# Threshold attention and an FNet mix on one core: the last 64 queries' scores in four 64x64 tiles, and the sequence transform's sine and cosine rest as two row tiles

## The chip, the cores and the metric

The kernel runs on one core of one Trainium2 chip, as one launch. The metric is the device time of that core in microseconds (us); lower is better. TensorE is called PE, VectorE DVE, ScalarE ACT, GpSimd POOL and SyncE SP, as the profile does. PE loads of stationary operands are listed apart, as PEld.

## The reference, cut to what matters

All tensors are fp32. `q`, `k` and `v` are (8 batches, 8 heads, 576 positions, 64); `tau` is 0.02.

```python
scores = (1 / sqrt(64)) * q @ k.T
scores = where(scores >= max(scores) - tau, scores, -1e9)
attn = exp(scores - max(scores));  attn = attn / (sum(attn) + 1e-9)
x = (attn @ v), heads side by side            # (8, 576, 512)
u = x + real(fft(fft(x, axis=1), axis=2))      # over the sequence, then over the features
ch = relu(layernorm(u) @ w_ch1) @ w_ch2        # 512 -> 2048 -> 512
return u + ch
```

## The kernel before, in words

There is no scheduler: every instruction stands in its engine's queue in the order in which the Python code issues it, and the code interleaves three streams by hand.

**Attention.** Two heads form a pair, 4 pairs to a batch, 32 in all. A pair's queries are taken in five steps `t` of a global index `i = 5 n + t`: four steps of 128 queries for each head, and a fifth (`t == 4`) with the last 64 queries of both heads. A step runs `scores` (PE), a softmax (DVE maximum `neg`, ACT exponential and threshold `thr`, DVE mask-and-sum, DVE `inverse`, and scaling by `den`), and one step later `weights_in_parts`, which transposes the weights `e` on PE into `pe` and `pw` and copies them by ACT into `ends` and `e_t`. At the steps 3 and 1 (of the next pair) `values_in_parts` multiplies by `v`. The first batch uses `step`, the second `second_batch`, and the other six a loop at the end with `softmax_first`, `softmax_second` and `softmax_third`. `prep_pair` transposes a pair's keys and queries on DVE at `t == 3` of the pair before; `prep_ends` fills `q_ends` on POOL; `load_v` loads the values by SP.

In the steps 0 to 3 the two heads lie on partitions 0 to 63 and 64 to 127 of `kT` and `qT`. A head's product contracts over 64 rows, so that it is a row tile, written 64*128 in the profile. In the first batch the four products of a step are issued head by head, later head 0 and head 1 in turns. In the fifth step `q_ends` is a 128x128 block diagonal of both heads' 64 queries, and its two products (one for each half of the keys) use the whole array (128*128).

Scores lie in PSUM in tiles `sc` of two banks, from a ring of two such tiles; all other PE results take one bank each from a ring of four, `mm`.

**Mixing.** `fold_rows` and `partial_sums` prepare the Fourier transform. `mixing(b)` then makes, for `u` in 0, 1, 2 (128, 48 and 128 sequence rows), the feature transforms `py`, evicted by ACT into `y_e` (cosine) and `y_o` (sine). `over_seq` then transforms over the sequence, in four products each: two with 128 rows of `y[:, 0]` and `y[:, 2]`, and two with the rest `y[:, 1]`, of which only 33 rows are not zero. For each of two column blocks `t`, ACT copies the sine side to `tmp`, and DVE makes the sum and the difference with the cosine side. `mixing` is a generator: each `yield` ends a piece.

**Channel product.** `channels` (the first group of 512 rows) and `two_level` (Strassen-like, the other eight) are generators too. `fill` takes pieces of them by a budget, and one piece of `mixing` by `mix(1)`, between the parts of an attention step. The last batch's mixing and the last two groups run after all attention has ended.

Each program matmul in fp32 that is no transpose leaves two MATMUL records and two LDWEIGHTS records in the trace.

Of the kernel before, what the change touches and what calls it, by code (L numbers as in the profile page):

```python
# [47 lines left out]
def kernel(  # L48
# [18 lines left out]
    NT = 5  # L67
# [75 lines left out]
    def load_v(n):  # L143

        b, p = n // NPAIR, PAIRS[n % NPAIR]
        vt = v_in[n % 2]
        for j in range(2):
            h = 2 * p + (j + p) % 2
            nc.sync.dma_start(
                out=vt[:, j:8:2, :], in_=v[b, h, 0:512, :].rearrange("(t p) d -> p t d", p=128)  # L150
            )
            nc.sync.dma_start(out=vt[64 * j : 64 * j + 64, 8 + j, :], in_=v[b, h, 512:576, :])
# [12 lines left out]
    for u in range(2):  # L165
        for j in range(2):
            nc.gpsimd.memset(v_in[u][64 - 64 * j : 128 - 64 * j, 8 + j, :], 0.0)


    q_ends = const.tile([128, 128], FP32, name="q_ends")  # L170
    nc.gpsimd.memset(q_ends[:, :], 0.0)
# [29 lines left out]
    seq_xe = const.tile([128, 2, NE], FP32, name="seq_xe")  # L201
    seq_xo = const.tile([128, 2, NO], FP32, name="seq_xo")


    SEQ = (
        (((0, 1, 128),), seq_even, 0, ((0, 128),)),
        (((0, 16, 128),), seq_odd, 1, ((0, 128),)),
        (((0, 129, 16), (16, 0, 1)), seq_xe, 0, ((0, 17),)),
        (((32, 0, 16),), seq_xo, 1, ((32, 16),)),
    )  # L210

    def load_seq():
        for u, (pieces, dst, parity, parts) in enumerate(SEQ):
            for p, r, n in pieces:
                nc.sync.dma_start(out=f[p : p + n, u, 0 : 2 * KH], in_=dft_seq[r : r + n, :])
            if dst is seq_xo:
                nc.sync.dma_start(out=f[32:33, u, KH : 2 * KH], in_=dft_seq[144:145, KH : 2 * KH])

    def copy_seq():
        nc.gpsimd.memset(seq_xe[:, :, :], 0.0)  # L220
        nc.gpsimd.memset(seq_xo[:, :, :], 0.0)
        for u, (pieces, dst, parity, parts) in enumerate(SEQ):
            for p, n in parts:
                for c in range(2):
                    nc.gpsimd.tensor_copy(
                        dst[p : p + n, c, :], f[p : p + n, u, KH * c + parity : KH * (c + 1) : 2]
                    )
        nc.gpsimd.memset(f[:, :, 145:160], 0.0)
        nc.gpsimd.memset(f[:, :, FW + 143 : FW + 160], 0.0)
# [153 lines left out]
    def inverse(i, nh):  # L383
        den = sb.tile([128, 2], FP32, tag="den", bufs=3, name="den")
        nc.vector.tensor_reduce(
            out=den[:, 0:nh], in_=den_eps[i % 3][:, 0:nh, :], axis=AXIS_X, op=ALU.add
        )
        nc.vector.reciprocal(den[:, 0:nh], den[:, 0:nh])  # L388
        return den

    heads = {}
    steps = {}
    xs = {}
# [7 lines left out]
    def prep_pair(n):  # L401

        q_raw, k_raw = loaded.pop(n)
        kT = sb.tile([128, D + S], FP32, tag="kT", name="kT")
        nc.vector.transpose(kT[:, D : D + S], k_raw[:, :])
        nc.vector.transpose(kT[64:128, 0:D], k_raw[64:128, 512:S])
        qT = sb.tile([128, S], FP32, tag="qT", bufs=1, name="qT")  # L410
        nc.vector.transpose(qT[:, :], q_raw[:, :])
        heads[n] = (qT, kT, v_in[n % 2])
        if n + 1 < B * NPAIR and not late:
            load_pair(n + 1)

    def prep_ends(n):

        for j in range(2):
            hp = slice(64 * j, 64 * j + 64)
            nc.gpsimd.tensor_copy(q_ends[hp, hp], heads[n][0][hp, 512:S])  # L420
# [6 lines left out]
    def scores(i):  # L427
# [3 lines left out]
        nh = 2 if t < 4 else 1  # L431
        sc = [ps.tile([128, 2, 512], FP32, tag="sc", name=f"sc{j}") for j in range(nh)]
        if t < 4:
            order = [(c, j) for c in range(2) for j in range(2)]
            if i < per_batch:
                order.sort(key=lambda cj: cj[1])
            for c, j in order:
                if True:
                    hp, k0 = slice(64 * j, 64 * j + 64), D * (1 - j)
                    nc.tensor.matmul(  # L440
                        sc[j][:, c, 0:HALF], qT[hp, 128 * t : 128 * t + 128],
                        kT[hp, k0 + HALF * c : k0 + HALF * (c + 1)], start=True, stop=True,
                    )
        else:
            for c in range(2):
                nc.tensor.matmul(  # L446
                    sc[0][:, c, 0:HALF], q_ends[:, :], kT[:, D + HALF * c : D + HALF * (c + 1)],
                    start=True, stop=True,
                )
        steps[i] = (sc, nh)  # L450

    def softmax(i, between=None, meanwhile=None, behind=None):


        t = i % NT
        sc, nh = steps[i]
        neg = sb.tile([128, 2], FP32, tag="neg", bufs=3, name="neg")
        thr = sb.tile([128, 2], FP32, tag="thr", bufs=3, name="thr")
        e = sb.tile([128, 2 * S], FP32, tag="e", name="e")
        for j in range(nh):  # L460
            nc.vector.tensor_reduce(  # L461
                out=neg[:, j : j + 1], in_=sc[j][:, :, 0:HALF], axis=AXIS_XY, op=ALU.max,
                negate=True,
            )
        if meanwhile is not None:
            meanwhile()
        for j in range(nh):
            ej = e[:, S * j : S * (j + 1)].rearrange("p (c n) -> p c n", c=2)
            nc.scalar.activation(
                out=ej, in_=sc[j][:, :, 0:HALF], func=ACT.Exp, bias=neg[:, j : j + 1], scale=1.0  # L470
            )
            if j == 0:
                nc.scalar.activation(
                    out=thr[:, 0:nh], in_=neg[:, 0:nh], func=ACT.Identity,
                    bias=thr_off[:, :], scale=-1.0,
                )
            nc.vector.scalar_tensor_tensor(  # L477
                out=ej, in0=sc[j][:, :, 0:HALF], scalar=thr[:, j : j + 1], in1=ej,
                op0=ALU.is_ge, op1=ALU.mult, accum_out=den_eps[i % 3][:, j, 0:1],
            )  # L480
# [4 lines left out]
        den = inverse(i, nh)  # L485
# [3 lines left out]
        if normalized(i // NT):  # L489
            nc.vector.tensor_scalar(  # L490
                out=e[:, 0:S], in0=e[:, 0:S], scalar1=den[:, 0:1], scalar2=None, op0=ALU.mult
            )
            if nh == 2:
                nc.scalar.activation(
                    out=e[:, S : 2 * S], in_=e[:, S : 2 * S], func=ACT.Copy, scale=den[:, 1:2]
                )
            steps[i] = (e, None)
        else:
            steps[i] = (e, den[:, 0:nh])

    def spread_inverse(i):
        e, den = steps[i]
        if i % NT == 4:
            nc.scalar.copy(e[:, S : S + 64], e[:, 512:S])
        if den is None:
            return
        nh = den.shape[1]
        rec = sb.tile([128, 2 * D], FP32, tag="rec", name="rec")
        nc.scalar.copy(
            rec[:, :].rearrange("p (j d) -> p j d", j=nh), _repeated(den, 2 * D // nh)  # L510
        )
        steps[i] = (e, rec)

    def softmax_first(i):
        sc, nh = steps[i]
        neg = sb.tile([128, 2], FP32, tag="neg", bufs=3, name="neg")
        thr = sb.tile([128, 2], FP32, tag="thr", bufs=3, name="thr")
        e = sb.tile([128, 2 * S], FP32, tag="e", name="e")
        for j in range(nh):
            nc.vector.tensor_reduce(  # L520
                out=neg[:, j : j + 1], in_=sc[j][:, :, 0:HALF], axis=AXIS_XY, op=ALU.max,
                negate=True,
            )
        for j in range(nh):
            ej = e[:, S * j : S * (j + 1)].rearrange("p (c n) -> p c n", c=2)
            nc.scalar.activation(  # L526
                out=ej, in_=sc[j][:, :, 0:HALF], func=ACT.Exp, bias=neg[:, j : j + 1], scale=1.0
            )
            if j == 0:
                nc.scalar.activation(  # L530
                    out=thr[:, 0:nh], in_=neg[:, 0:nh], func=ACT.Identity,
                    bias=thr_off[:, :], scale=-1.0,
                )
        steps[i] = (sc, nh, e, thr)

    def softmax_second(i):
        sc, nh, e, thr = steps[i]
        for j in range(nh):
            ej = e[:, S * j : S * (j + 1)].rearrange("p (c n) -> p c n", c=2)
            nc.vector.scalar_tensor_tensor(  # L540
                out=ej, in0=sc[j][:, :, 0:HALF], scalar=thr[:, j : j + 1], in1=ej,
                op0=ALU.is_ge, op1=ALU.mult, accum_out=den_eps[i % 3][:, j, 0:1],
            )
        steps[i] = (nh, e, inverse(i, nh))

    def softmax_third(i):
        nh, e, den = steps[i]
        for j in range(nh):
            nc.scalar.activation(  # L549
                out=e[:, S * j : S * (j + 1)], in_=e[:, S * j : S * (j + 1)], func=ACT.Copy,  # L550
                scale=den[:, j : j + 1],
            )
        if nh == 1:
            nc.scalar.copy(e[:, S : S + 64], e[:, 512:S])
# [6 lines left out]
    def weights_in_parts(i):  # L561
# [25 lines left out]
        nc.tensor.transpose(pe[:, 0, :], e[:, 512:640], ident[:, :])  # L587
# [6 lines left out]
        else:  # L594
            for j in range(2):
                hp = slice(64 * j, 64 * j + 64)
                nc.scalar.copy(ends[hp, 0:kept, q0 : q0 + 64], pe[hp, 0:kept, hp])
        qs = slice(q0, q0 + (128 if t < 4 else 64))
        for j in range(2 if t < 4 else 1):
# [3 lines left out]
            for c in range(4):  # L603
                c0 = (S + D) * j + 128 * c
# [3 lines left out]
            else:  # L608
                nc.scalar.copy(  # L609
                    e_t[:, :, qs].rearrange("p (j c) q -> p j c q", j=2),  # L610
                    pw[:, :, :].rearrange("p c (j q) -> p j c q", j=2),
# [1298 lines left out]
```

## Time and profile before

| | |
|---|---|
| time, three runs | 1544.44, 1545.87, 1548.71 us; median 1545.87 |
| the profiled execution: its own time | 1547.94 us |
| its span, first to last instruction | 1546.2 us |
| granted TensorE clock | 0.997 |
| busy: PE, PEld, DVE, ACT, POOL | 1524.0, 1186.0, 1063.2, 916.4, 779.4 us |
| PE groups the change touches: L440, L446 | 168.4 us in 1024 records, 36.3 us in 128 |
| L766 (`py`), L783 and L787 (`over_seq`) | 34.6 us in 240, 66.4 us in 320 |

"Busy" is the union of the records' durations. A matmul's record lasts longer than the time until the next can start, so that records overlap and a busy PE can still be slowed; what a piece of work costs PE is read from the start of its first record to the start of the next piece. "x8" in a line of the timeline merges eight records in a row; the time in brackets is idle time before the line and what ended it. The first batch of attention takes about 0 to 125 us, the second 125 to 320 us, and the others some 168 us each until 1313 us.

### The profile page before, as it was taken

To read this page: it belongs to the slowest core of one execution; us is meant where nothing else is said; L and a number is where in the kernel's file an instruction comes from. 1 tells how busy PE (TensorE), PEld (TensorE's weight loads), DVE (VectorE), ACT (ScalarE), POOL (GpSimd) and SP (SyncE) were. 2 spreads that over 40 slices of the span, in tenths; PEclk is the share of its full clock that TensorE was granted. 3 is DMA by queue.
4 is the path that set the end of the run, shared out by engine and by line. 5 is a ranking of instruction groups with operands and counts; after the bars stand their busy time and mean duration, and the time that the engine had idled before them with its cause. 6 is when DMAs were issued, how large, how long until landed. Compare 5 with 4: busy or idle time off the path is not lost.

```text
span 1546.2 us, 27021 instructions
## 1 busy us (share of the span) xinstructions
PE 1524.0 (99%) x9786; PEld 1186.0 (77%) x9786; DVE 1063.2 (69%) x2141; ACT 916.4 (59%) x1921; POOL 779.4 (50%) x964
## 2 busy tenths in 40 slices
PE   9999999999999999999999999999999999999999
PEld 5556555556788778887788878887788778989999
DVE  7977676846779466866578566956687657746546
ACT  6875676655666576656775666666665676133131
POOL 3775563034365642546255724554264625647635
PEclk9999999999999999999999999999999999999999
DMA  7423233465956354644455354635464534646655
GB/s 171 130 59 119 78 92 105 139 183 165 280 187 206 92 173 125 186 113 146 146 167 160 120 159 133 199 92 172 120 195 132 160 117 142 220 163 231 234 196 184
DMA packets 248907, 239.31 MB, mean 155 GB/s; under 512 B 197027, under 2 KB 218533, under 8 KB 228678
## 3 DMA queue, kind: packets, MB, share of 16 engines
q1 hardware_dynamic: 246262, 237.28, 50.1%
q8 instruction: 78, 1.28, 0.3%
q10 hardware_dynamic: 2512, 0.30, 0.1%
q14 instruction: 55, 0.45, 0.1%
HBM read 205.93 MB, written 31.46 MB: 154 GB/s over the span
## 4 chain that ended last, share of the span: by engine, by line
PE 91%; DVE 4%; ACT 2%; POOL 1%; DMA 1%; issue 0%; ACTq 0%; DVEq 0%; POOLq 0%
PE ph L1210 25%; PE po L1400 21%; PE pv L636 10%; PE sc L440 10%; PE pw L605 7%; PE po L933 4%; PE ph L909 3%; PE sc L446 2%; PE py L766 2%; PE pe L587 1%; PE pa L783 1%; PE pn L858 1%; PE pa L787 1%; PE pm L360 1%; PE po L1379 1%; DVE neg L461 1%
## 5 line engine op out<-in xcount | busy, mean ns | idle before, releaser
L520 DVE TENSOR_REDUCE neg<-sc 128x1 f32<-128x576 f32 x216 | 154.3, 751 | 117.1 <-PE sc L440 105.5
L526 ACT ACTIVATE e<-sc,neg 128x576 f32<-128x576 f32 x216 | 158.6, 734 | 114.3 <-DVE neg L520 114.3
L1147 DVE TENSOR_TENSOR hs<-ph,hs 128x512 f32<-128x512 f32 (+1 forms) x128 | 105.3, 823 | 167.1 <-PE ph L1210 97.3
L1400 PE MATMUL po<-w,w_all 128*128 128x128 f32 x1728 | 219.4, 276 | 0.0
L1400 PEld LDWEIGHTS po<-w,w_all 128*128 128x128 f32 x1728 | 205.4, 192 | 7.4 <-issue 4.0
L1156 POOL TENSOR_TENSOR w<-hs 128x512 f32<-128x512 f32 x32 | 42.1, 1317 | 312.3 <-ACT hs L1152 249.3
L540 DVE SCALAR_TENSOR_TENSOR e<-sc,thr,e 128x576 f32<-128x576 f32 x216 | 168.4, 812 | 27.2 <-ACT thr L530 27.1
L1210 PE MATMUL ph<-u_t,w 128*128 128x256 f32 x768 | 180.9, 382 | 0.6 <-DMA w<-f 0.6
L607 ACT COPY e_t<-pw 128x512 f32<-128x512 f32 x256 | 148.4, 594 | 44.2 <-PE pw L605 42.7
L440 PE MATMUL sc<-kT,qT 64*128 64x288 f32 x1024 | 168.4, 430 | 5.9 <-DVE e L477 5.5
L605 PE MATMUL pw<-ident,e 128*128 128x128 f32 x1152 | 169.3, 274 | 3.7 <-ACT ends L593 1.9
L549 ACT ACTIVATE e<-e,den 128x576 f32<-128x576 f32 x216 | 157.4, 774 | 2.9 <-DVE den L388 2.2
L1210 PEld LDWEIGHTS ph<-u_t,w 128*128 128x128 f32 x768 | 140.9, 190 | 23.6 <-issue 5.3
L1210 PE MATMUL ph<-w_all,w 128*128 128x256 f32 x672 | 157.1, 382 | 1.1 <-DVE w_all L1132 1.0
L605 PEld LDWEIGHTS pw<-ident,e 128*128 128x128 f32 x1152 | 135.8, 141 | 19.3 <-issue 5.6
L1263 POOL TENSOR_TENSOR w_all<-w_all 128x128 f32<-128x128 f32 (+2 forms) x160 | 121.7, 777 | 44.5 <-DVE w_all L1420 23.4
L1210 PEld LDWEIGHTS ph<-w_all,w 128*128 128x128 f32 x672 | 123.5, 190 | 23.9 <-issue 4.9
L1152 ACT ACTIVATE hs<-hs 128x512 f32<-128x512 f32 (+1 forms) x96 | 74.1, 772 | 113.8 <-DVE hs L1147 113.0
L440 PEld LDWEIGHTS sc<-kT,qT 64*128 64x128 f32 x1024 | 95.1, 186 | 55.4 <-issue 22.9
L1400 PE MATMUL po<-w,hs 128*128 128x128 f32 x912 | 119.8, 278 | 0.0
L1400 PEld LDWEIGHTS po<-w,hs 128*128 128x128 f32 x912 | 109.8, 192 | 9.5 <-issue 8.0
L636 PE MATMUL pv<-e_t,v_in 128*64 128x320 f32 (+1 forms) x512 | 72.1, 423 | 1.5 <-ACT e_t L609 0.8
(227 smaller groups left out, 2910.6 us busy)
## 6 DMA issues: line engine op xcount, KB each, us to landing
w<-f SPq DMA_DIRECT2D x150, 1024.0 KB, 4.9
hs<-in_moe_w_ch_dram SPq DMA_DIRECT2D x23, 512.0 KB, 4.7
q_in<-in_q_dram SPq DMA_DIRECT2D x128, 72.0 KB, 4.1
out_dram<-u SPq DMA_DIRECT2D x36, 256.0 KB, 2.5
k_in<-in_k_dram SPq DMA_DIRECT2D x124, 72.0 KB, 2.4
v_in<-in_v_dram SPq DMA_DIRECT2D x64, 128.0 KB, 5.1
f<-w SPq DMA_DIRECT2D x14, 512.0 KB, 3.3
f<-w SPq DMA_DIRECT2D x7, 1024.0 KB, 4.8
```

Source lines behind the costliest of these rows:

```text
L440: nc.tensor.matmul(sc[j][:, c, 0:HALF], qT[hp, 128 * t : 128 * t + 128], kT[hp, k0 + HALF * c : k0 + HALF * (c + 1)], start=True, stop=True,)
L520: nc.vector.tensor_reduce(out=neg[:, j : j + 1], in_=sc[j][:, :, 0:HALF], axis=AXIS_XY, op=ALU.max, negate=True,)
L526: nc.scalar.activation(out=ej, in_=sc[j][:, :, 0:HALF], func=ACT.Exp, bias=neg[:, j : j + 1], scale=1.0)
L540: nc.vector.scalar_tensor_tensor(out=ej, in0=sc[j][:, :, 0:HALF], scalar=thr[:, j : j + 1], in1=ej, op0=ALU.is_ge, op1=ALU.mult, accum_out ...
L549: nc.scalar.activation(out=e[:, S * j : S * (j + 1)], in_=e[:, S * j : S * (j + 1)], func=ACT.Copy, scale=den[:, j : j + 1],)
L605: nc.tensor.transpose(pw[:, c, :], e[:, c0 : c0 + 128], ident[:, :])
L607: nc.scalar.copy(e_t[:, 4 * j : 4 * j + 4, qs], pw[:, :, :])
L636: nc.tensor.matmul(pv[64 * j : 64 * j + 64, 0:m], vt[:, 2 * c + j, :], e_t[:, 4 * j + c, 0:m] if c < 4 else ends[:, 0, 0:m], start=(c == 0 ...
L1147: nc.vector.tensor_tensor(out=to, in0=bank, in1=to if other is None else other, op=ALU.add)
L1210: nc.tensor.matmul(bank[:, 256 * q : 256 * q + 256].rearrange("p (two n) -> p two n", two=2), left[:, 256 * c + 128 * q : 256 * c + 128 * ...
L1263: return lambda: eng.tensor_tensor(out=to, in0=to, in1=other, op=ALU.add)
L1400: nc.tensor.matmul(to, lefts[m][j][:, s], right_[:, 128 * s : 128 * (s + 1)], start=jn in (0, 4) and s == 0, stop=s == 3, skip_group_check ...
```

## The change

**The last 64 queries.** `q_ends` holds both heads' 64 queries one above the other, without the diagonal. Its four products, head `j` by key half `c`, each use 64 rows and 64 columns of the array and write partitions 64c to 64c + 63 of bank `j`. A query's scores are then in two halves on two partitions, so that maximum and sum are exchanged between the partition halves by small DVE reductions, and each step of the softmax runs twice on 288 columns instead of once on 576. `kT` holds the keys in a new order, with 32 of them double; the four products of the other steps have 256 or 320 columns instead of 288 each, and the values are loaded in the order that belongs to it.

**The sequence transform.** The rest `y[:, 1]` of the sine side is put on partitions 64 to 127 (its `py` now makes 128 stationary columns, not 48), and its two tables are joined into one, `seq_x`. For each column block the two rests, sine and cosine, are issued as two products over 64 rows each, and then the four products over 128 rows. The pieces of `mixing` are cut anew: both sides in one, and two empty pieces after the first block.

```diff
 load_v:
-            out=vt[:, j:8:2, :], in_=v[b, h, 0:512, :]...
-            out=vt[64 * j : 64 * j + 64, 8 + j, :], in_=v[b, h, 512:576, :]
+            for first, k0 in ((0, 320), (2, 0)):
+                out=vt[:, first + j : 8 : 4, :], in_=v[b, h, k0 : k0 + 256, :]...
+            out=vt[64 * j : 64 * j + 64, 8 + j, :], in_=v[b, h, 256:320, :]
 inverse:
+        if i % NT == 4:
+            parts = den_ends
+            exchange(parts[:, :, 2], parts[:, :, 0:1])
 prep_pair:
-        nc.vector.transpose(kT[:, D : D + S], k_raw[:, :])
-        nc.vector.transpose(kT[64:128, 0:D], k_raw[64:128, 512:S])
+        nc.vector.transpose(kT[:, 0:320], k_raw[:, 256:S])
+        nc.vector.transpose(kT[:, 352:672], k_raw[:, 0:320])
+        for j, k0 in ((0, 288), (1, 256)):
+            hp = slice(64 * j, 64 * j + 64)
+            nc.vector.transpose(kT[hp, 320:352], k_raw[hp, k0 : k0 + 32])
 prep_ends:
-        for j in range(2):
-            hp = slice(64 * j, 64 * j + 64)
-            nc.gpsimd.tensor_copy(q_ends[hp, hp], heads[n][0][hp, 512:S])
+        nc.gpsimd.tensor_copy(q_ends[:, :], heads[n][0][:, 512:S])
 scores:
+        order = [(c, j) for c in range(2) for j in range(2)]
+        if i < per_batch and t < 4:
+            order.sort(key=lambda cj: cj[1])
+        for c, j in order:
+            hp = slice(64 * j, 64 * j + 64)
+            if t < 4:
+                k0, k1 = ((64, 320), (352, 672), (0, 320), (352, 608))[2 * j + c]
+                to = sc[j][:, c, 512 - (k1 - k0) : 512] if c == 0 else sc[j][:, c, 0 : k1 - k0]
+                left = qT[hp, 128 * t : 128 * t + 128]
+            else:
+                k0, k1 = ((64, 352), (352, 640), (32, 320), (320, 608))[2 * j + c]
+                to, left = sc[0][64 * c : 64 * c + 64, j, 0:HALF], q_ends[hp, :]
+            nc.tensor.matmul(to, left, kT[hp, k0:k1], start=True, stop=True, ...)
-            for c in range(2):
-                nc.tensor.matmul(
-                    sc[0][:, c, 0:HALF], q_ends[:, :], kT[:, D + HALF * c : D + HALF * (c + 1)],
...
+    def maxima(i):            # t < 4: as before; t == 4:
+        nc.vector.tensor_reduce(out=own[:, :, 0], in_=both, axis=AXIS_X, op=ALU.max, negate=True)
+        exchange(own[:, :, 1], own[:, :, 0:1])
+        nc.vector.tensor_reduce(out=neg[:, :], in_=own[:, :, :], axis=AXIS_X, op=ALU.min)
+    def exchange(out_, in_):
+        for half in range(2):
+            a, b = 64 * half, 64 - 64 * half
+            nc.vector.tensor_reduce(out=out_[a : a + 64], in_=in_[b : b + 64], axis=AXIS_X, op=ALU.min)
 softmax, softmax_first, _second, _third: for t == 4 each of exponential, mask
   and scaling for j = 0 and 1 on 288 columns; the copy of 64 columns goes:
-            nc.scalar.copy(e[:, S : S + 64], e[:, 512:S])
 weights_in_parts, t == 4:
-                nc.scalar.copy(ends[hp, 0:kept, q0 : q0 + 64], pe[hp, 0:kept, hp])      # twice
+                for half in range(2):                                                  # four in all
+                    p0 = 64 * j + 32 * (1 - half)
+                    nc.scalar.copy(ends[p0 : p0 + 32, 0, q0 : q0 + 64],
+                                   pe[32 * j : 32 * j + 32, 0, 64 * half : 64 * half + 64])
+            if kept == 2:
+                nc.scalar.copy(ends[:, 1, q0 : q0 + 64], pe[:, 1, 0:64])
 mixing:
+                p0 = 64 if u == 1 and odd else 0
+                m, rows = p0 + n if p0 == 0 else 128, slice(p0, p0 + n)
-                        py[0:n, c0:c1], f[:, c, odd * FW + r : odd * FW + r + n],
+                        py[0:m, c0:c1], f[:, c, odd * FW + r - p0 : odd * FW + r - p0 + m],
-        def over_seq(y, odd, cols, m):     # four products: even 128, even rest, odd 128, odd rest
+        def rest_of_seq(y, rows, cols, m):
+            pa = ps.tile([128, 512], FP32, tag="mm", bufs=4, name="pa")
+            nc.tensor.matmul(pa[0:m, 0:KH], y[rows, 1, cols], seq_x[rows, :], start=True, stop=False, ...)
+        def over_seq(pa, y, odd, cols, m): # two products: even 128, odd 128
...
-            pb = over_seq(y_o, 1, cols, 128)
+            pb = rest_of_seq(y_o, slice(64, 128), cols, 128)
+            pa = rest_of_seq(y_e, slice(0, 64), cols, 128)
+            over_seq(pb, y_o, 1, cols, 128)
             nc.scalar.copy(sin, pb[:, 0:KH])
-            yield MIX / 11
-            pa = over_seq(y_e, 0, cols, 128)
+            over_seq(pa, y_e, 0, cols, 128)
...
-            yield MIX / 11
+            yield 2 * MIX / 11
+            if t == 0:
+                yield 0
+                yield 0
 load_seq, copy_seq: the rest of the table to partitions 0.. and 64.. of seq_x
   (six small DMAs and one row, four POOL copies), once at the start.
```

## The prediction

> **What bounds the kernel now.** I read the page first: spans, busy time, clock and the chain of waits.
>
> ```profile
> span 1546.2 us, 27021 instructions
> PE 1524.0 (99%) x9786; PEld 1186.0 (77%) x9786; DVE 1063.2 (69%) x2141; ACT 916.4 (59%) x1921; POOL 779.4 (50%) x964
> PEclk9999999999999999999999999999999999999999
> PE 91%; DVE 4%; ACT 2%; POOL 1%; DMA 1%; issue 0%; ACTq 0%; DVEq 0%; POOLq 0%
> ```
>
> PE is busy throughout at full clock and is 91% of the chain. So an edit is worth what it takes from PE's own sequence, and other engines count only where they make PE wait. Next, the waits: PE's largest is for the second buffer of scores, and it is small.
>
> ```profile
> PE sc L440 <- DVE e L477: 5.5, 7, 1.2
> ```
>
> Busy time hides what PE's tiles cost, so I read PE's timeline around a fifth step and around an ordinary one.
>
> ```profile
> 626.65 1.06 PE L1400 MATMUL po<-w,w_all 128*128 128x128 f32 x8
> 627.54 1.14 PE L446 MATMUL sc<-kT,q_ends 128*128 128x288 f32 x4
> 628.52 1.05 PE L1400 MATMUL po<-w,w_all 128*128 128x128 f32 x8
> ...
> 633.51 1.06 PE L1400 MATMUL po<-w,w_all 128*128 128x128 f32 x8
> 634.49 1.24 PE L440 MATMUL sc<-kT,qT 64*128 64x288 f32 x8
> 635.66 1.16 PE L1400 MATMUL po<-w,w 128*128 128x128 f32 x8
> 636.66 1.06 PE L1400 MATMUL po<-w,w_all 128*128 128x128 f32 x8
> ```
>
> From start to start, eight L1400 records take 0.89 us and the four L446 records 0.97 us (single records: 0.243 each, a slot). The eight records of L440 have as many columns each, and take 1.17 us, not 1.94: the two row tiles run side by side, four slots. But they cost a change of tiles: the L1400 ahead takes 0.98, not 0.89 (entry, 0.09); the group 1.17, not 0.97 (0.104 in the first slot, whose weight load nothing hides, and 0.09 at the exit); the L1400 behind 1.00, not 0.89 (its first weight load, 0.11). Together 0.40 us.
>
> **Part 1: the fifth step's scores, 32 times.** Before: 0.97 us, without a change of tiles. After: eight records of 288 columns in four tiles. Nothing in the trace is 64*64. The nearest rows are the row tiles above and the column tiles (128*64) of the values: 20 records of 320 columns in 2.85 us, where ten slots are 2.69, so two column tiles run side by side too, and a first load of 64 columns costs only 0.05. If both hold at once, the group is entry 0.09, two slots 0.486, first load 0.05, stagger 0.02, exit 0.09, next load 0.11: 0.85 us. Gain 0.12 x 32 = 3.9 us. Bounds: two at a time (four slots) loses 0.36 each, 11.6 us; a change of tiles for nothing would gain 0.47 each, 15 us. I take 3.9, because both pairs are rows and the price of the change shows on every group.
>
> Two rules of the Trainium skill can be held against this. "TensorE: Matmul & The Clock Gate", section "Measured speedup vs the span model", prices a pack at one matmul plus about 4 ns a tile, with no term for the change of tiles; by it the gain would be an estimated 15 us. The same page, section "The mechanism", says that matmuls start and end strictly in program order; then each tile's second record would hold back the next tile's first, the group would take an estimated five slots, and part 1 would lose. The trace disagrees with that order: in the first batch L440 is issued head by head, and still, at 75.35 us, the second head's first record starts 22 ns after the first head's, and the eight take 1.18 us to the next group.
>
> **Part 2: the other steps' scores.** 256 + 320 columns for one head, 320 + 256 for the other; 576 as before. Zero, if each row tile runs at its own pace. It does at 14.09 us: one head's records start at 0, 318, 561 and 803 ns, the other's at 738, 1055, 1298 and 1540.
>
> **Part 3: over the sequence, 16 blocks.** Before: two sides of eight records (L783, L787) at 0.123, 1.96 us. After: a row-tile pair of two slots 0.487, its change of tiles 0.40, and two sides of four records, 0.98: 1.87 us. Gain 0.09 x 16 = 1.5 us. Bounds: no overlap of the pair, 0.49 lost each; no price for the change, 0.49 gained. The block with one column stays at eight slots' worth.
>
> **Part 4: the sine side of `u` = 1.** Its 48 stationary columns are a tile change of their own:
>
> ```profile
> 841.47 0.64 PE L766 MATMUL py<-dim_s,f 128*48 128x128 f32 x4
> 842.03 0.33 PE L587 MATMUL pe<-ident,e 128*128 128x128 f32 x1
> 842.20 0.60 PE L605 MATMUL pw<-ident,e 128*128 128x128 f32 x4
> ```
>
> 0.56 us for four records that take 0.44 elsewhere, 0.09 at the entry, and 0.17 instead of 0.11 behind: 0.28 us. With 128 columns that goes. In six batches it stands alone (in the first and the last the cosine side beside it keeps the tile): 1.7 us.
>
> **Part 5: the softmax of the fifth step.** DVE: three small reductions for the maximum, 0.19 from start to start by L385's spacing, +0.57; two masks of 288, which I put at 0.50 + 0.08 by L540 (0.81 for 576) and L803 (0.46 for 289), +0.27; two small ones in `inverse`, +0.38. ACT: the first exponential is 0.23 shorter (0.50 for 0.73, by L643's 0.40 for 256). So scores are released some 0.6 us later (0.3 to 1.2 with the halves at their ends), `den` 1.0 later. With `kT`'s transposes (four for two, about +0.3) DVE gets 1.5 us a pair, ACT about 0.65 (two exponentials, two scalings, two to three more copies of 0.22 to `ends`, less one of 0.24).
>
> In the last 24 pairs this is covered: the fifth step's mask ends 2.4 us or more before the next scores (3.1 at 631.35 for 634.49), and its weights are ready 1.8 us or more before their transposes (median 3.0). The cover gone, each 0.1 us would cost 2.4 us in all. In the first eight it is not: at 35.27, 63.39, 121.09 and 204.70 the next scores' second head already waits for this mask (up to 4 x 0.6 = 2.4 us), and the values follow the copy to `e_t` (L609) by 0.05, 0.50, 0.29 and 0.07 us at 124.7, 172, 211 and 247, where 0.6 us of copies to `ends` go in ahead (up to 1.5 us). Between 0 and 3.9 I take 2.2, since a delay at one place gives slack at the next.
>
> **Part 6: the rest, at nothing.** SP issues two more loads of values a pair, 0.5 us each by the trace's DMA issues; behind them stand the weight loads (L1074), which wait 671 us for PE and for which PE waited 0.6 us in all. At the start three more small loads stand before the feature table and the second pair's values. POOL copies `q_ends` once, not twice (0.24 less). The wait of 0.3 us at the cosine side's first product for the sine copy (six batches, 1.9 us) moves to the bank that `pw` asks for; I count 0.6 gained, between 0 and 1.9. ACT's six waits for POOL at that copy (14.3 us) should shrink, off the path. In the tail PE waits 0.98 us at 1356.48 for DVE whatever comes before: 0.2 of part 3 is lost there.
>
> **Sum.** -3.9 - 1.5 - 1.7 + 2.2 - 0.6 + 0.2 = -5.3 us. The profiled execution (span 1546.2, 1.7 around it, 1547.94) becomes 1542.6; it lies 2.1 above the median of the runs, so the median 1545.87 becomes 1540.6.
>
> **The rivals.**
> *Two of four tiles at a time* (the slower end). Place: part 1. Four slots for two: +15.5 us on the forecast, 1556. Up to 2.5 slots part 1 still gains; from about 3.2 slots the whole is slower. For it: no 64*64 record exists. Against: both kinds of pair overlap fully. 0.10.
> *Row tiles in step.* Unequal products would run at the longer one's pace: four slots of 0.269 for 0.243, 0.104 x 128 = 13.3 us, 1554. Against: 14.09 us above. 0.05.
> *The softmax eats it.* The early waits cost all of 3.9, and late evictions behind the longer DVE work hold PE 0.1 us a pair: +4.1, 1544.7. For: DVE is 86% busy at 50 to 100 us. Against: the late slack. 0.12.
> *Not what it says:* the second rest's bank is not free, and the pair runs one after the other: +0.49 x 16 = 7.8, 1548.4. 0.02.
> *Better:* no give-back and the cosine wait gone: -9.0, 1536.9. 0.09.
> The forecast has 0.62, with its own range 1537 to 1544.
>
> **How the numbers follow.** A measurement of this kernel can tell about 0.3% (4.6 us) from no change, so faster is below 1541.2 and slower above 1550.5. The forecast lies near the edge: 0.43 of its 0.62 faster, 0.19 the same. Faster 0.43 + 0.09 = 0.52; same 0.19 + 0.12 (softmax) = 0.31; slower 0.10 + 0.05, and 0.02 for the serial pair with a bad run of other terms, 0.17. The range 1536 to 1549.5 leaves out the two upper rivals and the end of the best case.
>
> **What would show it.** Right: L446's successor takes about 0.65 us from its start to the next group, with starts of four tiles within some 25 ns, and 0.09 more on the record ahead; row-tile groups stay at 1.17 us; rest pairs at 0.68; PE waits rise only before 250 us. Wrong: slots of 64*64 beyond two, L440's group near 1.3, or new PE waits on DVE after 330 us.

## The result and the profile after

| | before | after |
|---|---|---|
| median of five runs | 1544.54 us (1543.24 to 1548.71) | 1556.82 us (1556.32 to 1562.92) |
| ratio, with its 95% interval | | 1.0085 [1.0062, 1.0109] |
| the profiled execution | 1547.94 us, span 1546.2 | 1556.32 us, span 1554.5 |

The change makes the kernel 0.85% slower, 12.3 us by the medians. The forecast was 1540.6 us, 0.26% faster, with a range that ended at 1549.5. It was wrong in size and in sign. One of the five runs of a later version, the spread exchange, took 1919.12 us at a granted clock of 0.753, and that version's median leaves it out.

PE itself did what was forecast. The page of the changed kernel, its lines for span, busy time and the chain of waits:

```profile
span 1554.5 us, 27560 instructions
PE 1518.9 (98%) x9834; PEld 1172.7 (75%) x9834; DVE 1097.5 (71%) x2430; ACT 932.6 (60%) x2017; POOL 768.5 (49%) x930
PE 76%; DVE 13%; ACT 4%; POOL 2%; DMA 2%; issue 2%; SPq 0%; ACTq 0%; DVEq 0%; POOLq 0%
```

PE is busy for 5.1 us less than before, but the span is 8.3 us longer: 13 us more without work for PE. PE's share of the chain falls from 91% to 76%, and DVE's rises from 4% to 13%. DVE has 289 instructions more and 34 us more to do.

PE's timeline in the changed kernel, around a fifth step, an ordinary step, and a pair of rests of the sequence transform (start, duration):

```profile
629.50 1.06 PE L1441 MATMUL po<-w,w_all 128*128 128x128 f32 x8
630.49 0.71 PE L453 MATMUL sc<-kT,q_ends 64*64 64x288 f32 x8
631.13 1.16 PE L1441 MATMUL po<-w,w_all 128*128 128x128 f32 x8
632.13 0.27 PE L612 MATMUL pe<-ident,e 128*128 128x128 f32 x1
...
637.28 1.24 PE L453 MATMUL sc<-kT,qT 64*128 64x256 f32 x8
638.45 1.16 PE L1441 MATMUL po<-w,w 128*128 128x128 f32 x8
...
1035.08 0.51 PE L816 MATMUL pa<-seq_x,y_o 64*128 64x289 f32 x1
...
1035.76 0.52 PE L824 MATMUL pa<-seq_even,y_o 128*128 128x145 f32 x2
```

The 64*64 group takes 0.64 us to the next group. The eight records ahead of it take 0.99 instead of 0.89, and the ones behind 1.00. So the four tiles run side by side, and with its change of tiles the group costs the 0.85 us that part 1 gave it. Products of 256 and 320 columns still take 1.17 us (part 2), and the pair of rests takes 0.68 (part 3). The rivals *two of four tiles at a time*, *row tiles in step* and *not what it says* are out. The first had 1556 us, next to what was measured, but that is chance: its cause is not there.

What is new are the waits. PE's list in the changed kernel up to 330 us (waited for: total us, times, longest):

```profile
PE sc L453 <- DVE e L510: 7.7, 10, 1.2
```

The head of the same list after 330 us:

```profile
PE pw L639 <- DVE w_all L1461: 3.5, 5, 0.9
PE ph L1251 <- DVE hs L1188: 2.9, 5, 1.6
PE py L801 <- ACT y_o L806: 2.2, 4, 0.6
PE po L1441 <- ACT w_all L1453: 1.4, 4, 0.4
```

Of these four waits the kernel before had two after 330 us:

```profile
PE ph L1210 <- DVE hs L1147: 2.1, 5, 0.8
PE pw L605 <- DVE w_all L1420: 0.2, 1, 0.2
```

None of the new late waits is for scores. They are for PSUM banks of the ring `mm` that an eviction has not yet freed: the channel product's `w_all` on DVE and on ACT, and the mixing's `y_o` on ACT. All three stand in the code behind a fifth step's softmax. (`hs` grows at one place only, behind the 55th step: 1.6 us there, 0.8 before.) To place the loss I compared the starts of all 160 score groups with those of before, interval by interval. Up to the 45th step the changed kernel loses 2.25 us, although the profile of before has two more stretches of 3.4 us at half clock there (up to 1.7 us lost in each). Of the rest, 6.13 us in all, +6.12 lies in five intervals: those that begin with the fifth step at which a batch's mixing is issued (every 20th step, called the mixing steps below). Another +1.87, three times 0.62, lies in intervals that begin with a batch's first step, where PE waits for ACT's `w_all`; and -2.3 in the three intervals that follow each mixing step, where the sequence transform lies.

One such mixing step in the changed kernel, a choice of the rows of PE, DVE and ACT (in brackets the idle time before a line and what ended it):

```profile
1011.98 0.72 PE L453 MATMUL sc<-kT,q_ends 64*64 64x288 f32 x8
1014.18 0.75 DVE L483 TENSOR_REDUCE own<-sc 128x2 f32<-128x576 f32 x1
1014.51 0.61 PE L801 MATMUL py<-dim_s,f 128*128 128x128 f32 x4
1014.96 0.31 DVE L494 TENSOR_REDUCE own<-own 64x2 f32<-64x2 f32 x2
1015.31 0.16 DVE L487 TENSOR_REDUCE neg<-own 128x2 f32<-128x4 f32 x1
1015.39 0.69 DVE L1461 TENSOR_TENSOR w_all<-w_all,po 128x512 f32<-128x512 f32 x1
1015.59 0.50 ACT L499 ACTIVATE e<-sc,neg 128x288 f32<-128x288 f32 x1 [2.42 <-DVE neg L487]
1015.99 0.28 ACT L504 ACTIVATE thr<-neg,thr_off 128x2 f32<-128x2 f32 x1
1016.14 0.66 PE L639 MATMUL pw<-ident,e 128*128 128x128 f32 x4 [0.91 <-DVE w_all L1461]
1016.17 0.49 ACT L499 ACTIVATE e<-sc,neg 128x288 f32<-128x288 f32 x1
1016.69 0.61 ACT L806 COPY y_o<-py 48x256 f32<-48x256 f32 x1
...
1017.35 0.94 PE L801 MATMUL py<-dim_c,f 128*128 128x65 f32 x6 [0.55 <-ACT y_o L806]
```

The same place before:

```profile
1007.08 1.14 PE L446 MATMUL sc<-kT,q_ends 128*128 128x288 f32 x4
1008.87 0.74 DVE L520 TENSOR_REDUCE neg<-sc 128x1 f32<-128x576 f32 x1
1009.54 0.67 DVE L1420 TENSOR_TENSOR w_all<-w_all,po 128x512 f32<-128x512 f32 x1
1009.71 0.74 ACT L526 ACTIVATE e<-sc,neg 128x576 f32<-128x576 f32 x1 [1.63 <-DVE neg L520]
1010.61 0.64 ACT L771 COPY y_o<-py 48x256 f32<-48x256 f32 x1
1010.66 0.60 PE L605 MATMUL pw<-ident,e 128*128 128x128 f32 x4
1011.29 0.94 PE L766 MATMUL py<-dim_c,f 128*128 128x65 f32 x6
```

From the start of the maximum, DVE's eviction starts after 1.21 us instead of 0.67, since three small reductions stand ahead of it; PE waits 0.91 us for its bank. The first exponential starts after 1.41 instead of 0.84, since it needs the exchanged maximum; ACT's copy of `y_o` behind the exponentials starts after 2.51 instead of 1.74, and PE waits another 0.55.

The small reductions are not the whole of that first wait. Counted from the start of the score group, the eviction ended at 3.13 us before, 0.45 ahead of PE's `pw` (3.58); now it ends at 4.10, 0.85 behind the moment at which PE is ready (3.25). Of this shift of 1.30 us the reductions make 0.54. PE comes 0.33 earlier by its own gains, and the maximum starts 0.41 later behind the scores (2.20 for 1.79), of which 0.14 is there without the exchange too (1.93).

### The profile page after: what moved, and what is told of

Its sections match the earlier page's. It is cut to its first block, busy times and chain, and to the rows that moved or that the text cites. A ratio compares the mean times of both kernels' runs of the same rounds, so it can differ in the third digit from the quotient of the medians.

```text
span 1554.5 us, 27560 instructions
## 1 busy us (share of the span) xinstructions
PE 1518.9 (98%) x9834; PEld 1172.7 (75%) x9834; DVE 1097.5 (71%) x2430; ACT 932.6 (60%) x2017; POOL 768.5 (49%) x930
## 4 chain that ended last, share of the span: by engine, by line
PE 76%; DVE 13%; ACT 4%; POOL 2%; DMA 2%; issue 2%; SPq 0%; ACTq 0%; DVEq 0%; POOLq 0%
PE ph L1251 24%; PE po L1441 17%; PE pv L669 9%; PE sc L453 9%; PE pw L639 6%; PE po L974 3%; DVE e L510 3%; PE ph L950 2%; ACT e L499 1%; DVE neg L475 1%; PE py L801 1%; DMA hs<-in_moe_w_ch_dram 1%; PE pa L824 1%; PE pm L359 1%; PE po L1420 1%
## 5 line engine op out<-in xcount | busy, mean ns | idle before, releaser
L499 ACT ACTIVATE e<-sc,neg 128x576 f32<-128x576 f32 (+1 forms) x320 | 220.2, 688 | 167.3 <-DVE neg L475 128.2
L510 DVE SCALAR_TENSOR_TENSOR e<-sc,thr,e 128x576 f32<-128x576 f32 (+1 forms) x320 | 229.0, 753 | 41.7 <-ACT thr L504 23.8
L475 DVE TENSOR_REDUCE neg<-sc 128x1 f32<-128x576 f32 x256 | 182.0, 751 | 103.5 <-PE sc L453 103.5
L453 PE MATMUL sc<-kT,qT 64*128 64x256 f32 (+1 forms) x1024 | 171.3, 431 | 9.2 <-DVE e L510 7.7
L578 ACT ACTIVATE e<-e,den 128x576 f32<-128x576 f32 (+1 forms) x240 | 161.8, 726 | 5.8 <-DVE den L393 5.5
L453 PEld LDWEIGHTS sc<-kT,qT 64*128 64x128 f32 x1024 | 110.9, 186 | 52.7 <-issue 25.2
```

Source lines behind the costliest of these rows:

```text
L453: nc.tensor.matmul(to, left, kT[hp, k0:k1], start=True, stop=True, skip_group_check=t == 4)
L475: nc.vector.tensor_reduce(out=neg[:, j : j + 1], in_=sc[j], axis=AXIS_X, op=ALU.max, negate=True)
L499: nc.scalar.activation(out=weights_of(i, e, j), in_=steps[i][j], func=ACT.Exp, bias=neg[:, j : j + 1], scale=1.0,)
L510: nc.vector.scalar_tensor_tensor(out=ej, in0=steps[i][j], scalar=thr[:, j : j + 1], in1=ej, op0=ALU.is_ge, op1=ALU.mult, accum_out=(den_en ...
L578: nc.scalar.activation(out=ej, in_=ej, func=ACT.Copy, scale=den[:, j : j + 1])
```

## The experiments

The theory that the first four tested is the queue theory: DVE's small reductions delay the evictions that stand behind them. Its rivals were the mixing theory (the pieces of `mixing`, cut anew, make the waits) and the tile theory (changes of tiles cost PE more than counted). Times are medians. Each difference is against the runs of before on the same chip, taken together with each group of versions: medians of 1545.26, 1545.72, 1543.95 and 1546.32 us for the four groups, in the order of the text.

**One part of the change at a time.** Each is the kernel before with one of the diff's two halves. The short diffs name what is taken over:

```diff
 sequence part alone (attention as before)
+    seq_x, rest_of_seq(...), over_seq(pa, ...), y_o's rest on rows 64 to 127, `yield 2 * MIX / 11`
 attention part alone (sequence transform as before)
+    q_ends of 64 columns, kT of S + 96, scores, maxima, exchange, masked, ends, load_v
```

> The kernel before with the sequence-transform part alone (joined table, row-tile rests, sine rest on partitions 64 up, pieces of the mixing recut). Queue theory (the loss comes from evictions that stand behind the fifth step's longer DVE and ACT work): the PE terms stand alone, -1.5 - 1.7 and up to -1.9 for the cosine wait, so 3 to 5 us faster than before, about 1540. Mixing theory (the recut pieces make the new waits): the waits of about 9 us seen around the mixing come with it, slower than before by 4 to 6 us, about 1550. Tile theory (changes of tiles cost more than their rows): 16 more changes, at most 2 us either way.

> The kernel before with the attention part alone (four 64x64 tiles, new key order, exchanged maxima and sums). Queue theory: all of the waits and none of the sequence gain, about 1560, 4 us above the changed kernel. Mixing theory: faster than before by about 2 to 4 us, 1541. Tile theory: about 1557, as the changed kernel.

Sequence part alone: 1543.58 us, -1.7 on before, ratio 0.9993 [0.9984, 1.0001]. Attention part alone: 1556.84, +11.6, ratio 1.0075 [1.0063, 1.0088]. The loss is all in the attention part, and the mixing theory falls. Lost clock is not the main part either: the attention part's two runs at a granted clock of 1.000 took 1555.43 and 1555.49 us, the five such runs of before 1543.46 to 1545.20. The sequence part gives less than forecast and can't be told from no change.

**The exchange left out, and doubled.**

```diff
 left out
-            exchange(parts[:, :, 2], parts[:, :, 0:1])
-        exchange(own[:, :, 1], own[:, :, 0:1])
-        nc.vector.tensor_reduce(out=neg[:, :], in_=own[:, :, :], axis=AXIS_X, op=ALU.min)
 doubled
-        for half in range(2):
+        for half in (0, 1, 0, 1):
```

> The changed kernel, but in the fifth step each partition half keeps its own maximum and its own sum: the two small exchanging reductions and the one that joins them are left out at the maximum, and the two at the sum, 0.5 and 0.3 us of DVE for each pair, also ahead of ACT's exponentials. PE's instructions are the same. Queue theory: the waits fall by half or more, 1546 to 1549. Tile and mixing theories: PE and the pieces are as in the changed kernel, so 1556 to 1557.

> The changed kernel with each exchange issued twice: 0.3 us more DVE at the maximum and 0.3 at the sum for each pair, all else the same. Queue theory: some 14 places where PE already waits get 0.3 to 0.6 us longer, 4 to 8 us slower than the changed kernel, 1561 to 1565. Tile and mixing theories: no change beyond 1 us, 1557.

Left out: 1544.1 us, -1.2 on before, ratio 0.9991 [0.9982, 1.0]. Doubled: 1570.38, +25.1, ratio 1.0158 [1.0145, 1.0172]. So the five small reductions of a pair, some 0.8 us of DVE, carry the whole loss, and four more cost another 13 us, where I expected 4 to 8. PE's tiles are the same in both, so the tile theory falls too. What this does not tell is why: the reductions occupy DVE, and they also make the exponentials wait. In the changed kernel the first exponential starts 1.38 us after the own maximum's start (median of 32), without the exchange 0.85, doubled 1.75.

**Queue or latency.** A second rival came up here, the latency theory: what counts is that the exponentials start late.

```diff
 the sum's exchange alone left out
-            exchange(parts[:, :, 2], parts[:, :, 0:1])
 idle reductions: no exchange, but as many reductions on scratch
-            out=own[:, :, 0], in_=both, axis=AXIS_X, op=ALU.max, negate=True
+            out=neg[:, :], in_=both, axis=AXIS_X, op=ALU.max, negate=True
-        nc.vector.tensor_reduce(out=neg[:, :], in_=own[:, :, :], axis=AXIS_X, op=ALU.min)
+        nc.vector.tensor_reduce(out=idle[:, :], in_=own[:, :, :], axis=AXIS_X, op=ALU.min)
-            exchange(parts[:, :, 2], parts[:, :, 0:1])
+            exchange(own[:, :, 1], own[:, :, 0:1])
```

> The changed kernel, but the fifth step's two small reductions that exchange the partial sums between the partition halves (in `inverse`) are left out: each half divides by its own half's sum. The three reductions for the maximum stay. Left out: half of each denominator of the last 64 queries. Queue theory (each small reduction delays whatever eviction stands behind it on DVE, wherever it stands): two of the five reductions go, so two fifths of the 12.7 us between this kernel and the one without any exchange, 1551 to 1553. Latency theory (what counts is that the exponentials of the fifth step start later, because they need the common maximum; sums are needed late and have slack): no change, 1556 to 1557.

> The kernel without the exchange (each half keeps its own maximum and sum, as before), with five small reductions put back at the same places on DVE, on scratch that nothing reads: three behind the own maximum, two ahead of the sum. Left out: the exchange of maxima and sums. Queue theory: the evictions behind them on DVE are as late as in the changed kernel, only ACT's exponentials can start some 0.5 us earlier; 1552 to 1557. Latency theory: nobody waits for these reductions, so as without the exchange, 1544 to 1547.

Without the sum's exchange: 1554.55 us, +8.8 on before, ratio 1.0058 [1.0044, 1.0071]. Idle reductions: 1548.89, +3.2, ratio 1.0025 [1.0016, 1.0034]. Both lie between the two theories' values. With the idle reductions DVE's queue is as full as in the changed kernel, yet two thirds of the loss are gone. PE's waits after 330 us with the idle reductions:

```profile
PE pw L641 <- DVE w_all L1463: 3.3, 5, 0.9
PE ph L1253 <- DVE hs L1190: 2.9, 5, 1.6
```

These waits for DVE's evictions are those of the changed kernel to 0.2 us. The wait for ACT's `y_o` is gone from the list: without the exchange it was 2.2 us, since PE came early; here PE is held by DVE first, and `y_o` is ready by then. The line without the exchange:

```profile
PE py L798 <- ACT y_o L803: 2.2, 4, 0.6
```

In the changed kernel, with later exponentials, PE waits for the one and then for the other. So each engine has its own share.

**The order changed.** If the evictions were the whole matter, it should help to issue them first.

```diff
 softmax_first(i), late fifth steps: own maximum only
-        for j in range(2):
-            exponentials(i, e, neg, thr, j)
 softmax_second(i), behind fill(True)
+        if i % NT == 4:
+            common_maximum(neg)      # the exchange and the minimum
+            for j in range(2):
+                exponentials(i, e, neg, thr, j)
 second version: the maximum's exchange on ACT, inverse(i) moved into softmax_third
+                nc.scalar.copy(own[a : a + 64, :, 1], own[b : b + 64, :, 0])
```

> The changed kernel with another order in the last 24 fifth steps: the own maximum is taken at once, but the exchange of maxima, and with it the exponentials, are issued only behind the portion of channel products that was issued behind them so far, so that the evictions of these products on DVE and ACT stand ahead of them. The same instructions, the same number. Queue theory: most of the late waits (some 8 us) go, the early 2 us stay: 1548 to 1552, unless the scores' buffer, released some 2 us later, comes too late for the next step; then about as before this edit, 1555. Latency theory: exponentials and mask are later by the whole portion, so slower still, 1560 or more.

> As the one with the evictions first, and in the last 24 fifth steps the exchange of maxima is two small copies on ACT instead of two reductions on DVE, and the exchange of the sums with the inverse is issued only just ahead of the scaling that uses it. Queue theory: the rest of the late waits on DVE goes too, with some 0.4 us more of ACT a step: 1546 to 1550, the best of the versions with an exchange. Latency theory: 1560 or more.

Evictions first: 1563.14 us, +17.4, ratio 1.0115 [1.0101, 1.0129]. Spread: 1569.18, +23.5, ratio 1.0154 [1.0141, 1.0168]. Both are slower than the change that they were to mend, as the latency theory says. PE's waits after 330 us with the evictions first:

```profile
PE py L810 <- ACT y_o L815: 6.8, 4, 1.7
...
PE po L1450 <- ACT y_o L815: 2.0, 1, 2.0
...
PE pw L648 <- DVE w_all L1470: 1.2, 4, 0.4
```

DVE's part did shrink, from 3.5 to 1.2 us, as wanted. But the exponentials, put off to 2.5 us in the last 24 fifth steps (median), push ACT's `y_o` behind them, and PE's wait for it grows from 2.5 us (2.2 and 0.3, at two places in the code) to 8.8.

**ACT's eviction ahead of the softmax, and later exponentials alone.** The combined theory: about a third of the loss is DVE's queue, and two thirds are ACT's evictions, late behind late exponentials.

```diff
 mixing first: late loop
+        if i % per_batch == 4 and mixes:
+            mix(1)
         softmax_first(i)
 ...
-        if mixes:
+        if mixes and i % per_batch != 4:
             mix(1)
 late exponentials: no exchange, and in exponentials(), t == 4, j == 0
+            nc.scalar.copy(idle[:, 0:2], neg[:, :])
+            nc.scalar.copy(idle[:, 2:4], neg[:, :])
```

> The changed kernel with one move: at each of the late mixing steps (every twentieth step, a fifth step) the mixing's portion of products and its copy on ACT (`y_o`) is issued ahead of the fifth step's softmax, not behind it. Same instructions. Combined theory (about a third of the 12.7 us is DVE's queue, and two thirds are ACT's evictions that stand behind exponentials which start some 0.5 us later): `y_o` no longer stands behind them, so most of the 6.1 us that these six steps lose goes: 1550 to 1553. If instead the exponentials' lateness counts through the mask and the release of the scores, nothing goes: 1556 to 1558. If PE only waits at the next copy of the ring, 1554 to 1556.

> The kernel without the exchange (each half keeps its own maximum and sum), with two small idle copies on ACT ahead of each fifth step's first exponential, on scratch that nothing reads: DVE's queue is as without the exchange, but the exponentials start some 0.4 us later. Left out: the exchange of maxima and sums. Combined theory: the larger share of the loss comes back without any small reduction on DVE, +4 to +7 on the kernel without the exchange: 1548 to 1551. Queue theory (DVE alone): 1544 to 1546.

Mixing first: 1551.37 us, +7.4 on before, ratio 1.0046 [1.0034, 1.0058], as the combined theory had it. The five mixing steps together now stand at +0.02 us against before, where the changed kernel has +6.12; nothing else moved by more than a microsecond. PE's waits after 330 us, the head of the list:

```profile
PE ph L1251 <- DVE hs L1188: 2.9, 5, 1.6
PE po L1441 <- DVE w_all L1461: 2.2, 4, 0.7
```

The waits for `y_o` are gone. Those for DVE's `w_all` at four of the mixing steps are shorter (2.2 us, 3.1 in the changed kernel), and one stretch at half clock that the changed kernel's profile has there (last section, up to 1.7 us) is missing. So the gain is not ACT's share alone.

Late exponentials: 1546.41, +2.5, ratio 1.0015 [1.0006, 1.0024]. That was below the combined theory's range, but the two copies overlap and put the exponentials off by only 0.13 us, a quarter of the exchange's 0.53. It stands 3.7 us above the version without an exchange, but with 1.4 us either way on each of the two it was too weak a test, so I made a stronger one:

```diff
+            nc.scalar.activation(
+                out=idle[:, :], in_=idle[:, :], func=ACT.Copy, scale=neg[:, 0:1]
+            )      # idle is 128x448
```

> The two small idle copies before turned out to put the exponentials off by only 0.13 us (0.98 for 0.85 from the own maximum's start; the changed kernel: 1.38), so this one has in their place one idle copy of 128x448 on ACT ahead of each fifth step's first exponential, some 0.5 us, which needs the own maximum but which nothing reads. DVE's queue is as without the exchange. Left out: the exchange of maxima and sums. Combined theory (lateness of the exponentials on ACT is the larger share, about 8 of 12.7 us): 1550 to 1553. If lateness alone is cheap and only both together are dear (PE waits twice in a row at the same place), 1546 to 1549.

1552.64 us, +6.3 on before, ratio 1.0042 [1.0028, 1.0056]. The first exponential starts at 1.37 us, as in the changed kernel. PE's waits after 330 us:

```profile
PE py L803 <- ACT y_o L808: 4.2, 4, 1.0
PE ph L1253 <- DVE hs L1190: 2.4, 5, 1.1
PE pw L641 <- DVE w_all L1463: 1.1, 3, 0.4
```

With this the account closes within the noise. Against the kernel without an exchange (-1.2 on before), DVE's reductions alone cost 4.4 us and later exponentials alone 7.5, together 11.9; the change itself stands 13.5 above it, and its attention part alone 12.8. The 95% intervals on before are 1.4 us either way for the version without an exchange and for the idle reductions, 2.2 for the later exponentials, 1.9 for the attention part and 3.6 for the change, so the shares are rough. Part of the 7.5 is clock: in the profile of the later exponentials the five mixing steps cost 0.5, 0.5, 0.5, 2.4 and 2.4 us more than without the exchange, and the last two have a stretch at half clock (last section). The other reading on record for that run, that only both together are dear, falls: each is dear by itself.

None of these versions beats both kernels. The best, the sequence part alone, can't be told from before.

## Why the prediction was wrong, step by step

**Parts 1 to 3: right.** The tiles cost what was forecast, to 0.01 us a group by the medians. The rule from the Trainium skill ("TensorE: Matmul & The Clock Gate", section "Measured speedup vs the span model") that counts no change of tiles would have put the group at two slots and some 4 ns for each further tile, an estimated 0.50 us. It is 0.64 here, and 0.21 more on its neighbours.

**Parts 3, 4 and 6 together: about half.** They were to bring 3.6 us. Alone they bring 4.6 in the profiled span (1541.5), but 1.7 by the medians. Of the 4.6, 1.5 lie before the 45th step, where the profile of before had three stretches of 3.4 us at half clock and this one had one; the late part is 3.1.

**Part 5: the step that failed.** It said that in the last 24 pairs the longer softmax "is covered", because the mask ends 2.4 us before the next scores and the weights are ready 1.8 us before their transposes. That cover held: every wait for `sc` in the changed kernel lies before 330 us, and no late wait for the transposes is for the weights. But that asks only who reads the softmax's results. It does not ask what stands behind the softmax in DVE's and ACT's own queues. Both engines evict PSUM banks of a ring of four, in program order, and PE ran within a few tenths of a microsecond of that ring: at the place shown above, `w_all` was evicted 0.45 us and `y_o` 0.04 us before PE went on. So 0.54 us more on DVE's queue and 0.77 on ACT's are not hidden there. The exponential "0.23 shorter" was misleading as well: two exponentials of 288 end later than one of 576, and ACT's `y_o` starts 1.95 us after the maximum even without the exchange, 1.74 before.

**The sum, in spans.** Forecast 1540.9 (1542.6 less 1.7 around it), measured 1554.5: 13.6 us off. By the intervals between score groups, the exchange costs 8.9 us after the 45th step (changed kernel against that without it), where the forecast had nothing. It costs 3.55 before, where I took 2.2 for the whole longer softmax, between 0 and 3.9. The other 3.4 us are missing even without the exchange: a span of 1542.1, where the forecast less its give-back is 1538.7. In the mixing steps PE came earlier and waited: they stand at +0.97 there instead of below nothing. That is about 1 us; where the rest went stays open, and by the medians more is missing (-1.2 on before, where the forecast without the give-back was -7.5).

**The rival.** *The softmax eats it* named this mechanism, with 0.12, and priced it at 0.1 us a pair. In the 18 late fifth steps that are no mixing steps the exchange costs 1.38 us in all, 0.08 on average, but twelve of them cost nothing and three cost 0.56, 0.41 and 0.21. At the five mixing steps it costs 5.15 us: 0.55 to 0.80 at four of them and 2.46 at the one with the stretch at half clock. Some 0.6 more lies in each of three intervals that open a batch. The price was an average over pairs that are not alike.

**What would show it.** "New PE waits on DVE after 330 us" was named as a sign of being wrong, and it is what came.

## What to carry to other kernels

Before a longer chain is called covered, list for each engine that it uses what is queued behind it until the next slack, and compare the delay with what the PSUM ring can spare there, place by place; who reads the chain's result is only half of the question. When an in-order queue has to carry small extra work, first move the evictions that PE is about to need ahead of the whole chain; here, splitting the chain around them only moved the wait to the next engine. A gain in PE's own time makes PE arrive earlier at the same evictions (0.33 us at the place shown), so part of it can come back as waiting.

## What the runs showed of the hardware that was not expected

Lost clock came along with short waits. Two windows of the changed kernel around the mixing step above (us; then busy time with records for PE, PEld, DVE, ACT, POOL; granted clock, DMA share, GB/s):

```profile
1013.00:1017.00 4.00, 2.89 (x24) 2.41 (x23) 3.27 (x9) 1.55 (x6) 1.75 (x2) 1.00 0.45 75
1017.00:1021.00 4.00, 3.65 (x21) 3.65 (x22) 1.67 (x9) 3.62 (x9) 0.00 (x0) 0.66 0.48 77
```

PE was idle for 1.1 of 4 us, in pieces of at most 0.91, and then ran at half clock for 3.4 us (1018.3 to 1021.7), up to 1.7 us lost; that interval lost 2.78 us where the other mixing steps lost 0.40 to 1.14. With the exponentials later alone it happened at two mixing steps (1014.9 and 1185.6, 2.7 us lost at each), with the evictions first and with the spread exchange at two late places each, and with the doubled exchange at one. The profiles of before, of the sequence part alone and of the version without the exchange show it only before 210 us or at the very end. In all eight late cases PE's records fill 41 to 59% of the 3.4 us ahead. But such waits alone do not decide it: at the last mixing step of the changed kernel PE waited just as long (0.89 and 0.56 us, busy for 2.85 of the 4 us from 1184.4) and kept full clock, and the attention part alone has no late stretch. What decides is not shown. The Trainium skill ("TensorE: Matmul & The Clock Gate", section "HAM oscillation — how this bites in real kernels") warns of idle gaps above some 3.4 us; here no idle piece ahead of the stretch was above 0.91 us.

The other point is what tiny instructions cost: a reduction of 64x2 takes 0.16 us on DVE, start to start, against 0.75 for 128x576. Two small copies on ACT that depend on the same operand overlap so far that they put the next instruction off by 0.13 us, not by twice the 0.19 that each is listed with.
